# A fused attention and mixture-of-experts kernel: the last segment's maximum, the late loads, the zero fills and the written-out order are changed

## The chip, the cores and the metric

The kernel runs on one core of a Trainium2 chip. The metric is the device time of one execution in microseconds (us). Its engines are TensorE (PE; its weight loads are PEld), VectorE (DVE), ScalarE (ACT), GpSimd (POOL) and SyncE (SP, which issues the loads and stores). Each engine works through its own queue in order.

## The reference

The input is x, 4 batches of 11456 tokens with 128 channels, float32. First comes an attention with 32 inducing points, then a mixture of 8 experts with 4 slots each, in which every token goes to every slot with a weight ("soft" routing).

```python
def mab(q, kv):
    s = scale * (q @ kv.transpose(0, 2, 1))
    s = s - s.max(-1, keepdims=True)
    a = np.exp(s)
    a /= a.sum(-1, keepdims=True) + 1e-09
    return a @ kv
h = mab(I, x)                       # per batch: 32 inducing points look at the tokens
x = mab(x, h)                       # tokens look at the 32 rows of h
...
logits = x @ phi                    # tokens x 32 slots
d = np.exp(logits - logits.max(0)); d /= d.sum(0) + 1e-09
slot_input = d.T @ x                # softmax over all tokens of all batches
h = np.maximum(slot_input[e] @ w1[e], 0.0); slot_out[e] = h @ w2[e]
c = np.exp(logits - logits.max(1)); c /= c.sum(1) + 1e-09
return c @ slot_out                 # softmax over the slots
```

## The kernel before

The 4 batches are cut into 6 tiles each, so there are 24 tiles n of up to 15 blocks of 128 tokens; names below carry the tile's number. Work goes in three passes.

**First pass, per tile.** x is loaded twice (L282, L294): `xn` as it lies and `xt` transposed (tiles 0 to 5 are transposed on TensorE instead). TensorE multiplies `xt` with the inducing points (s1p, L329), VectorE takes maxima, ScalarE exponentiates, VectorE transposes in 32 x 32 blocks (e1), and TensorE accumulates exp(s)·x per batch (ha, L405). After a batch's six tiles, `first_out` normalises to h (hs, htp, hts, bdg; L453 to L476).

**Second pass, `second(n)` per tile.** Scores of tokens against h (s2p, L329, needs `xt` again), VectorE transposes them (bts, L576) and takes the maximum over the 32 (bmx, L579), GpSimd subtracts it (`bt_n`, L583), ScalarE exponentiates (L586), TensorE transposes back (tt, L592) and multiplies with h·phi (lp, L605), which gives the logits and their divisor; VectorE divides into the logit buffer l_all (L624, the last block by ScalarE, L629/L631), and GpSimd multiplies `bt` with the reciprocal divisor (bml, L635).

**Segments.** Three tiles make a segment k (`segment(k)`, L661). Its maximum over all tokens is taken on VectorE (t1_k, L667; in the last two segments tile by tile, tm, L657), turned by TensorE (pt_k, L672), reduced (mc_k, L679), spread to all partitions by TensorE (pb_k, L682) and copied by ScalarE (m_all, L685). d_n = l − maximum is taken on VectorE for the tiles in the list DV, straight from pb_k, on GpSimd for the others, from the copy (L706); ScalarE exponentiates it (L709), and TensorE accumulates exp(d)ᵀ·bt over the segment into u_k (L719). DW lists the tiles whose d is written in the pair layout that the l_all reads have, the others in a plain one. Since each segment has its own maximum, the sums of the segments are weighted against each other afterwards (ws, wl; L777 to L822).

**Experts (`experts()`, L752).** From the u_k come the slot inputs (sit, L845 to L852, copied into the zero-filled buffer ma by z1s, L863), 128 products with w1 (hpm, L872), ReLU on ScalarE (L880), a transpose per half (htm, L885), copies on VectorE into the zero-filled ma and mb (z2, L890), 128 products with w2 (so, L901), the divisor (zpp, rz; sos, L908), and the result spread to all partitions (sr, L911; srs, L914). The zero fills are two memsets on GpSimd (L764 of 1440 columns, L774 of 1152). The weights (8 transfers of 960 KB and one of 512 KB, L741, L743) are the last loads.

**Third pass, `third(n)` and `output(n)`.** The softmax over slots on the logits (maxima cm, L511; subtraction, L517/L520; exponential, L524; half sums ch, L532; sums cz, L541 to L547; product and transpose, L967, L970), then products with srs (po, L1000), copies to ot by VectorE and ScalarE (L1011), and stores (L1020).

Small zero products (`fill`, L1057 to L1063, and L235) keep TensorE working at some places. The large x and weight tiles share a ring of 13 buffers; some x tiles lie instead in parts of l_all that are not yet written (XTAG, NTAG), and the first logits there wait until such a tile is used up. Each step is registered by `op(engine, cost, name, function, ...)`, and the order in which the steps are issued, on all engines and the DMA queue, is written out by hand as a string of pairs of characters (ORDER, L54), one pair per step. So nothing decides the order at build time, and each engine's queue is a subsequence of that string.

## Time and profile before

| | |
|---|---|
| runs | 217.27, 216.47, 216.58 us; median 216.58 |
| profiled execution | 217.6 us, of which the span of instructions is 215.5 |
| busy, share of the span | TensorE 188.7 us (88%), VectorE 162.6 (75%), ScalarE 135.5 (63%), GpSimd 125.5 (58%) |
| HBM | 49.84 MB read, 23.59 MB written, 341 GB/s over the span |

The span begins at 0 with the first instruction; all positions below are in us from there. "PEclk" is the share of full clock that TensorE was granted. A share of busy time over the whole span mixes stages, so the rows below go by stretches of time. Where a row says [0.65 <-ACT d L709], the engine was idle for 0.65 us ahead of it, and ScalarE's step at L709 ended that.

### The profile page before, as it was taken

What the parts mean: (1) busy time and instruction counts of PE and PEld (TensorE: products, weight loads), DVE (VectorE), ACT (ScalarE), POOL (GpSimd) and SP (SyncE); (2) the same over time, 40 slices, a digit from 0 to 9 for tenths busy, and PEclk for the clock granted to TensorE, in tenths of its full rate; (3) what the DMA queues carried; (4) which work ended last, traced back from release to release, by engine and by line L of the source; (5) the groups of instructions that cost most, each with busy time, mean ns of one, the idle gap of its engine ahead of it and who ended that gap; (6) DMA issues with size and microseconds to landing.
All of it is one profiled execution on the core that took longest, in us unless ns stands there. A gap on an engine that the chain in (4) does not pass through costs nothing.

```text
span 215.5 us, 6873 instructions
## 1 busy us (share of the span) xinstructions
PE 188.7 (88%) x2778; PEld 129.7 (60%) x2778; DVE 162.6 (75%) x375; ACT 135.5 (63%) x368; POOL 125.5 (58%) x138
## 2 busy tenths in 40 slices
...
GB/s 218 387 429 416 393 422 415 415 415 361 233 389 422 422 412 419 408 419 412 415 416 414 419 236 0 6 5 3 66 378 410 418 421 422 412 421 423 411 416 190
DMA packets 12799, 73.87 MB, mean 343 GB/s; under 512 B 1633, under 2 KB 2657, under 8 KB 12769
## 3 DMA queue, kind: packets, MB, share of 16 engines
...
q10 hardware_dynamic: 432, 0.17, 0.3%
...
HBM read 49.84 MB, written 23.59 MB: 341 GB/s over the span
## 4 chain that ended last, share of the span: by engine, by line
PE 59%; DMA 10%; DVE 9%; POOL 7%; issue 4%; ACT 3%; SPq 1%; DVEq 0%; ACTq 0%; POOLq 0%
PE po L1000 10%; PE s1p L329 9%; PE ha L405 9%; PE s2p L329 7%; DMA w<-w 6%; PE lp L605 6%; DMA xn<-xn 4%; DVE ot L1011 4%; PE tt L592 4%; PE tp L306 3%; POOL d L706 3%; PE hpm L872 2%; POOL bt L583 2%; PE u L719 2%; DVE l_all L970 2%
## 5 line engine op out<-in xcount | busy, mean ns | idle before, releaser
L1000 PE MATMUL po<-l_all,srs 32*128 32x480 f32 (+1 forms) x200 | 43.6, 746 | 3.8 <-DVE l_all L970 1.8
L1000 PEld LDWEIGHTS po<-l_all,srs 32*128 32x128 f32 x200 | 22.0, 229 | 24.4 <-ACT ot L1011 10.5
L1011 ACT COPY ot<-po 128x480 f32<-128x480 f32 (+1 forms) x65 | 31.8, 576 | 7.4 <-PE po L1000 7.1
L583 POOL TENSOR_TENSOR bt<-bt,bm 128x480 f32<-128x480 f32 x24 | 23.6, 1001 | 16.6 <-DVE bm L579 14.1
L967 POOL TENSOR_TENSOR ct<-ct,cz 128x480 f32<-128x480 f32 x24 | 23.7, 996 | 9.2 <-DVE cz L547 9.2
L605 PE MATMUL lp<-bdg,a2t 128*128 128x132 f32 x192 | 25.7, 278 | 0.6 <-ACT d L709 0.6
L340 DVE TENSOR_SCALAR_CACHE_REDUCE s<-s1p 128x480 f32<-128x480 f32 (+1 forms) x24 | 15.0, 644 | 14.2 <-PE s1p L329 13.8
L635 POOL TENSOR_TENSOR bt<-bt,bz 128x480 f32<-128x480 f32 x24 | 23.5, 1003 | 2.8 <-DVE bz L617 1.9
L605 PEld LDWEIGHTS lp<-bdg,a2t 128*128 128x128 f32 x192 | 23.3, 190 | 1.8 <-ACT d L709 0.8
L1011 DVE COPY ot<-po 128x480 f32<-128x480 f32 (+1 forms) x35 | 20.2, 602 | 3.3 <-PE po L1000 3.3
L706 POOL TENSOR_TENSOR d<-l_all,m_all 128x512 f32<-128x512 f32 x19 | 21.8, 1173 | 1.3 <-ACT m_all L685 1.3
L520 POOL TENSOR_TENSOR ct<-l_all,cm 128x512 f32<-128x512 f32 x18 | 18.8, 1053 | 3.9 <-DVE l_all L970 2.4
L405 PE MATMUL ha<-xn,e 128*32 128x128 f32 x570 | 19.6, 275 | 1.6 <-issue 1.5
L329 PE MATMUL s1p<-xt,it_sb 128*32 128x480 f32 x160 | 19.8, 571 | 0.8 <-ACT xt L314 0.7
L386 ACT ACTIVATE s<-s,negm 128x480 f32<-128x480 f32 (+1 forms) x24 | 16.6, 697 | 5.7 <-DVE negm L371 5.7
L329 PE MATMUL s2p<-xt,hts 128*32 128x480 f32 x160 | 19.6, 571 | 0.0
L405 PEld LDWEIGHTS ha<-xn,e 128*32 128x32 f32 x570 | 16.5, 109 | 4.1 <-issue 2.2
L709 ACT ACTIVATE d<-d 128x512 f32<-128x512 f32 x24 | 14.9, 633 | 5.9 <-POOL d L706 5.0
L342 POOL MEMSET s<- 128x16 f32 x4 | 0.5, 117 | 31.1 <-DVE e L389 30.8
L970 DVE STREAM_TRANSPOSE l_all<-ct 128x480 f32<-128x480 f32 x24 | 15.8, 660 | 1.9 <-POOL ct L967 1.9
L389 DVE STREAM_TRANSPOSE e<-s 128x480 f32<-128x480 f32 x24 | 15.6, 657 | 1.9 <-ACT s L386 1.7
L576 DVE STREAM_TRANSPOSE bt<-s2p 128x480 f32<-128x480 f32 x24 | 15.6, 665 | 0.8 <-PE s2p L329 0.4
...
## 6 DMA issues: line engine op xcount, KB each, us to landing
...
```

The source lines that it names most:

```text
L329: nc.tensor.matmul(dst[32 * g : 32 * g + 32, :w], lhs, src, start=True, stop=True)
L386: nc.scalar.activation(t[:, :v], t[:, :v], AF.Exp, bias=T["negm", b, g], accum_out=z6[:, a : a + 1])
L405: nc.tensor.matmul(ha[32 * q : 32 * q + 32, :P], T["e1", a][:, j * S : (j + 1) * S], T["xn", a][:, j * P : (j + 1) * P], start=c == lo and ...
L520: nc.gpsimd.tensor_tensor(t.rearrange("p (a e s) -> p a e s", s=S, e=2), l_blocks(n), m, op=ALU.subtract)
L583: nc.gpsimd.tensor_tensor(t, t, T["bm", n][:, :nb].unsqueeze(2).broadcast_to(full), op=ALU.subtract)
L605: nc.tensor.matmul(pt[:, q * 4 * SZ : (q * 4 + m) * SZ], t[: m * S, q * P : (q + 1) * P], bdgs[b % 2].rearrange("p q s -> p (q s)")[: m * ...
L635: nc.gpsimd.tensor_tensor(t, t, T["bz", n][:, :nb].unsqueeze(2).broadcast_to(full), op=ALU.mult)
L706: e.tensor_tensor(t.rearrange(o, s=S, e=2), l_pairs(n), m, op=ALU.subtract)
L967: nc.gpsimd.tensor_tensor(t, t, T["cz", n][:, :nb].unsqueeze(2).broadcast_to([P, nb, S]), op=ALU.mult)
L970: nc.vector.transpose(l_of(n), T[ck][:, :w])
L1000: nc.tensor.matmul(ptile("mm", ("po", n, g, h))[:, : hi - lo], T["srs",][q, :], l_of(n)[q, lo:hi], start=True, stop=True)
L1011: (nc.vector.tensor_copy if dve else nc.scalar.copy)(T["ot", n][:, g * w + lo : g * w + hi], T["po", n, g, h][:, : hi - lo])
```

## The change

- **Last segment.** The column maxima mc_k are kept for all segments. Before pb_7 is spread, a new reduction on VectorE (nmc) takes the largest of all eight, so that pb_7 holds the maximum over all tokens. d_21, d_22 and d_23 subtract that; the copy m_all for segment 7 and the reduction nm go, the weights wl (now on VectorE, 64 wide, from pb_7) no longer cover segment 7, and u_7 is copied without a weight.
- **Subtractions.** d_20 goes from VectorE to GpSimd (DV); d_20 and d_22 are written in the plain layout (DW).
- **Zero fills.** Both go from GpSimd to ScalarE, as a product of ones with 0.
- **Loads.** xt_12 lies at the end of l_all instead of in the ring. 28 transfers (HS: xt 9 to 11 and 18 to 23, xn 6 and 14 to 23, w 0 to 7) are issued as two halves of 480 KB each.
- **Experts.** Each half of hpm and so is written as experts 0 to 3 and 4 to 7 instead of 0 to 5 and 6 to 7.
- **Fills on TensorE.** 13 zero products instead of 10: one early, five between u_17 and pt_7, three between u_18 and pb_7, two behind sit, two ahead of sr.
- **Order.** ORDER is another string. The loads keep their order; the compute steps and the stores do not.

The rest of the diff (a variant for tiles in a list XB, which is empty, and the host's reshaping) moves nothing.

```diff
-DV = [12, 20, 21, 22, 23]
-DW = [3, 9, 14, 20, 22]
+DV = [12, 21, 22, 23]
+DW = [3, 9, 14]
-XTAG = {9: 'xa', 10: 'xb', 15: 'xa', 16: 'xb'}
+XTAG = {9: 'xa', 10: 'xb', 15: 'xa', 16: 'xb', 12: 'xc'}
-NF = 10
+HS = [('t', 9), ('t', 10), ('t', 11), ('n', 6), ('t', 18),
...
+NF = 13
 ORDER = (
...
+                    for r in halves(("n", a)):
+                        nc.sync.dma_start(t[:, r], xn[a - 1][:, r])
...
-            nc.vector.tensor_reduce(stile("mc", ("mc", k))[:S], T["pt", k][:S, :w], axis=AX.X, op=ALU.max)
+            nc.vector.tensor_reduce(mc_all[:S, k : k + 1], T["pt", k][:S, :w], axis=AX.X, op=ALU.max)
...
+            mc = mc_all[:S, k : k + 1] if k < NSEG - 1 else T["nmc",][:S]
+            nc.tensor.matmul(ptile("mm", ("pb", k))[:, :S], mc.broadcast_to([S, P]), ident[:S, :S], start=True, stop=True)
...
+        def g1():
+            nc.vector.tensor_reduce(stile("nmc", ("nmc",), 1, 1)[:S], mc_all[:S], axis=AX.X, op=ALU.max)
...
-            nc.gpsimd.memset(ma[:, : 5 * ZW], 0.0)
+            nc.scalar.mul(ma[:, : 5 * ZW], ones.broadcast_to([P, 5 * ZW]), 0.0)
...
-            nc.gpsimd.memset(T["z2", 1], 0.0)
+            nc.scalar.mul(mb[:, : 4 * ZW], ones.broadcast_to([P, 4 * ZW]), 0.0)
...
         def g2():
-            nc.gpsimd.tensor_tensor(
-                blocks(stile("w2", ("wl",), W * S, 1)), blocks(m_last), T["nm",].unsqueeze(1).broadcast_to([P, W, S]), op=ALU.subtract,
-            )
+            pb = T["pb", NSEG - 1][:, :S].unsqueeze(1).broadcast_to([P, W, S])
+            nc.vector.tensor_tensor(blocks(stile("w2", ("wl",), W * S, 1)), blocks(m_last), pb, op=ALU.subtract)
...
         def g5():
-            nc.vector.tensor_tensor(us_all[:, last], T["u", NSEG - 1][:, :S], T["wl",][:, (W - 2) * S : (W - 1) * S], op=ALU.mult)
+            (nc.vector.tensor_copy if G5 == "DVE" else nc.scalar.copy)(us_all[:, last], T["u", NSEG - 1][:, :S])
...
-        parts = (range(0, 6), range(6, E))
+        parts = (range(0, 4), range(4, E))
```

How the order moves is seen at three places. The first is GpSimd's queue around the first step of tile 18: `bt` is scores less maximum (L583, then L616) or times reciprocal (L635, then L682), `d` is logits less segment maximum. Before:

```order
L635 TENSOR_TENSOR bt_15_1503<-bt_15_1503,bz_15_1793 128x480
L635 TENSOR_TENSOR bt_16_1584<-bt_16_1584,bz_16_1869 128x480
L635 TENSOR_TENSOR bt_17_1661<-bt_17_1661,bz_17_1886 128x480
L583 TENSOR_TENSOR bt_18_1939<-bt_18_1939,bm_18_1942 128x480
L706 TENSOR_TENSOR d_13_1974<-l_all_78,m_all_79 128x512
L706 TENSOR_TENSOR d_14_1976<-l_all_78,m_all_79 128x8x32x2
L583 TENSOR_TENSOR bt_19_1954<-bt_19_1954,bm_19_1958 128x480
L583 TENSOR_TENSOR bt_20_1956<-bt_20_1956,bm_20_1960 128x480
L774 MEMSET mb_2096 128x1152
L583 TENSOR_TENSOR bt_21_2068<-bt_21_2068,bm_21_2072 128x480
L583 TENSOR_TENSOR bt_22_2070<-bt_22_2070,bm_22_2076 128x480
L583 TENSOR_TENSOR bt_23_2074<-bt_23_2074,bm_23_2078 128x480
```

With the change:

```order
L682 TENSOR_TENSOR bt_14_1547<-bt_14_1547,bz_14_1776 128x480
L682 TENSOR_TENSOR bt_16_1626<-bt_16_1626,bz_16_1849 128x480
L682 TENSOR_TENSOR bt_17_1701<-bt_17_1701,bz_17_1903 128x480
L775 TENSOR_TENSOR d_13_1945<-l_all_78,m_all_79 128x512
L775 TENSOR_TENSOR d_14_1992<-l_all_78,m_all_79 128x8x32x2
L616 TENSOR_TENSOR bt_18_1980<-bt_18_1980,bm_18_1982 128x480
L616 TENSOR_TENSOR bt_19_1984<-bt_19_1984,bm_19_1988 128x480
L616 TENSOR_TENSOR bt_20_1986<-bt_20_1986,bm_20_1990 128x480
L682 TENSOR_TENSOR bt_15_1549<-bt_15_1549,bz_15_1778 128x480
L616 TENSOR_TENSOR bt_21_2050<-bt_21_2050,bm_21_2101 128x480
L616 TENSOR_TENSOR bt_22_2103<-bt_22_2103,bm_22_2105 128x480
L682 TENSOR_TENSOR bt_18_1980<-bt_18_1980,bz_18_2108 128x480
```

d_13 and d_14 now stand ahead of bt_18, the product of tile 15 behind bt_20, the memset of mb is gone, and the subtractions and products of tiles 18 to 23 are interleaved.

The second is TensorE's queue at the same time, where pt_4, pb_4 are the turned and the spread maximum of segment 4 (tiles 12 to 14). Before:

```order
L605 MATMUL lp_17_1880<-bdg0_88,a2t_17_1860 128x132 x3
L605 MATMUL lp_17_1880<-bdg0_88,a2t_17_1860 128x99
L672 MATMUL pt_4_1888<-cst_70,t1_4_1872 32x128
L329 MATMUL s2p_18_1899<-xt_18_911,hts_3_1876 32x480 x4
L719 MATMUL u_3_1836<-d_10_1653,bt_10_1002 32x32 x15
L329 MATMUL s2p_19_1919<-xt_19_913,hts_3_1876 32x480 x4
L719 MATMUL u_3_1836<-d_11_1733,bt_11_1117 32x32 x15
L682 MATMUL pb_4_1944<-cst_70,mc_4_1897 128x32
```

With the change:

```order
L727 MATMUL pt_4_1896<-cst_70,t1_4_1855 32x128
L640 MATMUL lp_17_1898<-bdg0_89,a2t_17_1846 128x132 x3
L640 MATMUL lp_17_1898<-bdg0_89,a2t_17_1846 128x99
L481 MATMUL htp_3_1905<-cst_70,hs_3_1894 128x128
L738 MATMUL pb_4_1915<-cst_70,mc_all_80 128x32
L788 MATMUL u_3_1736<-d_10_1694,bt_10_1020 32x32 x15
L346 MATMUL s2p_18_1950<-xt_18_965,hts_3_1921 32x480 x4
```

pt_4 now stands ahead of lp_17, and pb_4 ahead of s2p_18.

The third is ScalarE's queue at the end of the chain, from d_21's exponential on. Before:

```order
L709 ACTIVATE d_21_2376<-d_21_2376 128x512
L709 ACTIVATE d_22_2380<-d_22_2380 128x512
L709 ACTIVATE d_23_2382<-d_23_2382 128x512
L819 ACTIVATE wl_2389<-wl_2389 128x96
L728 COPY us_all_82<-u_6_2313 128x32
L880 ACTIVATE ma_2391<-hpm_0_2468 128x128
L524 ACTIVATE ct_8_2510<-ct_8_2510 128x480
```

With the change:

```order
L778 ACTIVATE d_21_2401<-d_21_2401 128x512
L778 ACTIVATE d_22_2403<-d_22_2403 128x512
L778 ACTIVATE d_23_2405<-d_23_2405 128x512
L884 ACTIVATE wl_2408<-wl_2408 128x64
L799 COPY us_all_83<-u_6_2331 128x32
L836 ACTIVATE ma_2470<-ones_87 128x1440
L540 ACTIVATE ct_9_2480<-ct_9_2480 128x480
```

The copy of pb_7 (further up) is gone, and the zero fill of ma, read from ones, stands behind us_6's copy and ahead of the exponentials of the third pass.

## Rows read from the trace of the kernel before

**Rows 1.** Stretches: length, busy PE, PEld, DVE, ACT, POOL (instructions), clock, DMA share, GB/s.

```profile
12.00:104.00 92.00, 91.82 (x1516) 64.31 (x1518) 78.86 (x192) 61.26 (x178) 52.98 (x56) 1.00 0.99 400
...
117.00:139.00 22.00, 21.42 (x444) 16.71 (x443) 21.50 (x45) 17.48 (x54) 21.72 (x23) 1.00 0.47 190
139.00:154.00 15.00, 13.50 (x351) 11.48 (x348) 12.26 (x32) 4.83 (x15) 12.40 (x17) 0.89 0.02 4
...
160.00:200.00 40.00, 36.91 (x150) 18.27 (x144) 30.86 (x65) 32.27 (x74) 24.63 (x26) 0.74 1.02 417
```

**Rows 2.** Timeline of the DMA queue: start, us, what, count.

```profile
54.52 0.33 SPq L294 DMA_DIRECT2D l_all<-xt  x1
```

**Rows 3.** Timeline of GpSimd: start, us, what, count, idle before.

```profile
116.94 1.00 POOL L583 TENSOR_TENSOR bt<-bt,bm 128x480 f32<-128x480 f32 x1 [0.90 <-DMA w<-w]
118.22 2.31 POOL L706 TENSOR_TENSOR d<-l_all,m_all 128x512 f32<-128x512 f32 x2 [0.28 <-ACT m_all L685]
...
122.36 1.07 POOL L774 MEMSET mb<- 128x1152 f32 x1
...
135.82 2.93 POOL L635 TENSOR_TENSOR bt<-bt,bz 128x480 f32<-128x480 f32 x3
...
139.02 1.32 POOL L764 MEMSET ma<- 128x1440 f32 x1
```

**Rows 4.** Timeline of TensorE, 104 to 147 us.

```profile
108.98 1.84 PE L405 MATMUL ha<-xn,e 128*32 128x128 f32 x57
...
114.34 1.01 PE L329 MATMUL s2p<-xt,hts 128*32 128x480 f32 x8
...
116.65 0.40 PE L682 MATMUL pb<-cst,mc 32*128 32x32 f32 x2
...
139.68 0.89 PE L719 MATMUL u<-d,bt 128*32 128x32 f32 x60 [0.65 <-ACT d L709]
...
142.10 4.61 PE L872 MATMUL hpm<-w,ma 128*32 128x128 f32 x112
146.64 0.33 PE L885 MATMUL htm<-cst,ma 128*128 128x128 f32 x1
```

**Rows 5.** Timeline of VectorE, 124 to 139 us.

```profile
124.53 1.70 DVE L667 TENSOR_REDUCE t<-l_all 128x32 f32<-128x1536 f32 x1
...
136.94 0.69 DVE L706 TENSOR_TENSOR d<-l_all,pb 128x512 f32<-128x512 f32 x1 [0.42 <-ACT m_all L685]
137.55 0.26 DVE L811 TENSOR_REDUCE nm<-m_all 128x32 f32<-128x96 f32 x1
137.72 1.60 DVE L706 TENSOR_TENSOR d<-l_all,pb 128x512 f32<-128x512 f32 x2
```

**Rows 6.** Timeline of ScalarE, 138 to 141 us.

```profile
138.91 1.16 ACT L709 ACTIVATE d<-d 128x512 f32<-128x512 f32 x2 [0.61 <-DVE d L706]
...
140.14 0.16 ACT L728 COPY us_all<-u 128x32 f32<-128x32 f32 x1
```

**Rows 7.** Groups of ScalarE by shape: busy us, mean ns, idle before.

```profile
L709 ACT ACTIVATE d<-d 128x512 f32<-128x512 f32 x24 | 14.9, 633 | 5.9 <-POOL d L706 5.0 <-DVE d L706 0.6 <-POOL s L342 0.2
...
L785 ACT ACTIVATE mb<-mb 128x192 f32<-128x192 f32 x1 | 0.4, 375 | 0.0
```

**Rows 8.** Busy time by stretch, around the experts and first stores.

```profile
141.50:144.90 3.40, 3.40 (x60) 2.98 (x61) 3.40 (x8) 0.00 (x0) 3.25 (x5) 0.50 0.03 7
144.90:146.70 1.80, 1.80 (x65) 1.60 (x58) 0.43 (x1) 1.22 (x3) 1.80 (x2) 1.00 0.00 0
158.00:166.00 8.00, 7.61 (x42) 3.84 (x42) 7.49 (x17) 7.77 (x20) 4.29 (x5) 1.00 1.02 408
```

**Rows 9.** Timeline of all engines after the experts.

```profile
151.64 0.35 DVE L908 TENSOR_SCALAR sos<-so,rz_l 128x128 f32<-128x128 f32 x1 [0.15 <-PE so L901]
...
153.68 0.89 ACT L1011 COPY ot<-po 128x240 f32<-128x240 f32 x3 [0.84 <-PE po L1000]
```

**Rows 10.** Groups by shape, VectorE.

```profile
L511 DVE TENSOR_REDUCE cm<-l_all 128x16 f32<-128x512 f32 x24 | 15.8, 660 | 0.0
```

More of the change, by code (lines that the diff above doesn't have):

```diff
@@ L79, with tw, gw @@
 FREE_RINGS = ()
-DYN = ("mm", "half", "x")
+DYN = ("mm", "half", "x", "a2t")
 def width(n):
     return SIZES[n % NCH] * S
+def tw(n):
+    return LW if n in XB else width(n)
+def gw(n):
+    return [LW, LW, LW, LW - P] if n in XB else [width(n)] * 4
 def valid(n):
@@ L276, in load, with halves @@
         assert not {tag_of("xn", a), tag_of("xt", a)} & taken
+        def halves(n):
+            w = XW // 2 if n in HS else XW
+            return [slice(o, o + w) for o in range(0, XW, w)]
         def ldn(lo, hi):
@@ L289, in load @@
         for lo, hi in zip(cuts, cuts[1:]):
[L290 removed]
+            op("DMA", 2.50 * (hi - lo) / 2048 + 0.05 * (("n", a) in HS) + (1.9 if a == 0 and not lo else 0.0), ("ldn", a, lo), ldn(lo, hi), (), [("xn", a, lo)], [] if lo else [(tag_of("xn", a), ("xn", a))])
         if a in HOST_T:
             def ldt():
[L294 to L296 removed]
+                t = xtile("xt", a)
+                for r in halves(("t", a)):
+                    nc.sync.dma_start(t[:, r], xt_d[HOST_T.index(a)][:, r])
+            op("DMA", 2.50 * nb / 16 + 0.05 * (("t", a) in HS), ("ldt", a), ldt, (), [("xt", a)], [(tag_of("xt", a), ("xt", a))])
             return
@@ L503, in soft @@
     def soft(pre, n, src, half, key):
-        w, nb = width(n), SIZES[n % NCH]
-        full = (P, nb, S)
+        w, nb = tw(n), tw(n) // S
         mk, zk = (pre + "m", n), (pre + "z", n)
@@ L562, in a2_of @@
     def a2_of(n):
-        return T["bt", n][:, : width(n)]
+        return T["bt", n][:, : tw(n)]
     def second(n):
@@ L576, in bts, with bcp, btx @@
             nc.vector.transpose(wtile("s2", ("bt", n))[:, :w], T["s2p", n][:, :w])
+        def bcp():
+            t = wtile("a2t", ("s2c", n), LW)
+            nc.scalar.copy(t[:, :sw], T["s2p", n][:, :sw])
+            nc.scalar.copy(t[:, sw:], T["s2p", n][:, sw - S : sw])
+        def btx():
+            pt = ptile("mm", ("tx", n))
+            for q in range(4):
+                nc.tensor.transpose(pt[:, q * P : (q + 1) * P], T["s2c", n][:, q * P : (q + 1) * P], ident)
         def bmx():
-            nc.vector.tensor_reduce(stile("bm", ("bm", n), JM, RINGS["bm"])[:, :nb], blocks(a2_of(n)), axis=AX.X, op=ALU.max)
+            src = T["tx", n] if n in XB else a2_of(n)
+            nc.vector.tensor_reduce(stile("bm", ("bm", n), LW // S, RINGS["bm"])[:, :nb], blocks(src), axis=AX.X, op=ALU.max)
         def bsb():
+            if n in XB:
+                if ("xbt",) not in T:
+                    btile("x", ("xbt",))
+                i = XB.index(n)
+                T["bt", n] = T["xbt",][:, i * LW : (i + 1) * LW]
             t = blocks(a2_of(n))
-            nc.gpsimd.tensor_tensor(t, t, T["bm", n][:, :nb].unsqueeze(2).broadcast_to(full), op=ALU.subtract)
+            e, src = (nc.vector, blocks(T["tx", n])) if n in XB else (nc.gpsimd, t)
+            e.tensor_tensor(t, src, T["bm", n][:, :nb].unsqueeze(2).broadcast_to(full), op=ALU.subtract)
         def bxp():
@@ L960, in third @@
     def third(n):
-        w, nb = width(n), SIZES[n % NCH]
+        w, nb = tw(n), tw(n) // S
         ck = ("ct", n)
@@ L988, in output @@
     def output(n):
-        w = width(n)
+        ws = gw(n)
+        w, at = ws[0], [sum(ws[:g]) for g in range(5)]
         cuts = [0, w // 2, w] if n == HEAD else [0, w]
         parts = list(zip(cuts, cuts[1:]))
+        assert n != HEAD or n not in XB
         for h, (lo, hi) in enumerate(parts):
@@ L1094 @@
             xt[HOST_T.index(a), :, : nb * P] = part.transpose(3, 0, 2, 1).reshape(C, nb * P)
-    def cut(t):
-        return np.ascontiguousarray(t.reshape(-1, P, H, XW // H).transpose(0, 2, 1, 3))
     w1 = inputs["moe_w1"].transpose(1, 0, 2)
```

187 lines of the change are left out of this document (108 added, 79 removed).

## The prediction

> **What bounds the kernel now.** I read the stages first, then the engine timelines of the stretch where no stage is full, then the clock. The busy times by stretch [rows 1] show three stages. From 12 to 104 us TensorE works 91.82 of 92.00 us and the DMA engines are at 0.99, so both are full; the change takes no product out of that stage, so nothing can be won there, and a stall of TensorE would add one for one. From 160 to 200 us the stores run at 1.02 of the DMA engines and 417 GB/s; the bytes stay, so that stage only starts earlier or later. Between lies a chain: the DMA share falls to 0.47 (117 to 139 us) and to 0.02 (139 to 154 us). What is won or lost there moves the stores and so the end.
>
> In the chain GpSimd is busy 21.72 of 22.00 us from 117 to 139 [rows 1]: from bt_18 at 116.94 to the last of the bt·bz products at 135.82 + 2.93 = 138.75 [rows 3], 21.81 in all. VectorE is the second candidate: its last two subtractions (1.60 from 137.72) release ScalarE's last two exponentials, which end at 138.91 + 1.16 = 140.07 [rows 5, 6]. u_23 waits for that; `u` ends at 139.68 + 0.89 = 140.57, and the experts' first product comes at 142.10 [rows 4]. So before the change the VectorE-ScalarE chain ends last, 1.3 us behind GpSimd. Whoever shortens it by more meets GpSimd.
>
> **The change part by part.**
>
> *Loads.* 28 transfers are cut in two, and xt_12 goes to the end of the logit buffer. The queue still stops at xt_15, issued at 54.52 once s2p_9 has left its place in that buffer [rows 2], which is not changed; and TensorE is full meanwhile. I cost this part at 0, the 28 further issues (0.33 each on a queue that mostly waits) with it. The cover: loads have no gain to give while TensorE is the bound, and the weights, last in the queue, are first needed at 142. What speaks against it is the rate: halves of the same size in the stores, 158 to 166 us, moved at 408 GB/s [rows 8] beside 417 [rows 1], 2.2% less. On the 20 halved x loads (20 × 0.98 MB at 417 GB/s = 47 us) that is 1.0 us of lateness. From 117 us on 22 × 190 GB/s = 4.2 MB come [rows 1], 10 us at full rate, so the 8.39 MB of weights end at 127 and the last x tile lands 20 us before, at 107; the products of the last two tiles run from 108.98 [rows 4], so 2 us are to spare and 1.0 costs nothing. The Trainium skill ("DMA: Bandwidth & Descriptors", its rule on batching) asks for at least 1 MiB per transfer for three quarters of the peak, which speaks against halves; taken as a quarter lost on those 47 us (an estimate from that page), the last x tile would come some 14 us too late and the sum be 230. This case's 960 KB transfers lie under that size too and move at 417 GB/s, so the rows decide.
>
> *Zero fills.* The fill of 1152 columns (GpSimd, 1.07) [rows 3] goes to ScalarE far earlier, where ScalarE is busy 61.26 of 92.00 us [rows 1]; it stands ahead of an exponential and of hs_2, and would cost up to its own length if TensorE waited for hs_2. I take 0. The fill of 1440 columns goes from GpSimd (1.32) [rows 3] to ScalarE, behind the last exponentials. No row shows such a fill on ScalarE. 192 columns took 0.375 and 512 took 0.633 [rows 7], 0.81 ns per column, which carried on gives 0.633 + 928 × 0.81 ns = 1.38. Below stands GpSimd's 1.32, above a price in proportion, 0.633 × 1440/512 = 1.78. I take 1.38, as the two rows are ScalarE's own.
>
> *GpSimd in the chain.* From bt_18 on it loses the fill (1.07) and d_13 and d_14 (2.31 [rows 3], now ahead of bt_18), and gains the product of tile 15 (0.98) and d_20 (1.16): 21.81 − 1.07 − 2.31 + 0.98 + 1.16 = 20.57. But the maximum t1_5 (1.70 on VectorE at 124.53 [rows 5]) now stands ahead of bts_21, so bt_21 and its neighbours come late. Counted through the two orders with the row durations, GpSimd idles about 1.9 (0 if VectorE is ahead, 2.8 if every bt waits). pb_4, now ahead of s2p_18, I put at about 114, so that d_13 and d_14 (2.31, and 0.3 to 0.5 for the copy) leave bt_18 at 116.85. GpSimd's end: 116.85 + 20.57 + 1.9 = 139.3, 0.55 later than before.
>
> *VectorE and ScalarE in the chain.* Gone ahead of d_23: nm (0.26) [rows 5], the copy of pb_7 that d_21 waited for (0.42 of idle) [rows 5], d_20 (0.91, as d_22 now: 1.60 − 0.69) less a transpose of 0.66 (an estimate from a cm of the same width [rows 10]) that takes its place (0.25), and 0.2 by which the plain layout shortens d_22 (0.91 to 0.69 [rows 5]). Added: the new maximum over 8 numbers, 0.2 (bounds 0.1 and the 0.26 of nm). So d_23's exponential ends at 140.07 − 0.26 − 0.42 − 0.25 − 0.2 + 0.2 = 139.1. u_23 then waits for GpSimd: 139.3 + 0.45 (half of `u`'s 0.89) = 139.75, 0.8 earlier than 140.57. us_7 no longer waits for the weight, which is worth about 0.1. The fill of 1440 ends at 139.1 + 0.23 (two short steps, which end at 140.30 now [rows 6]) + 1.38 = 140.7, about when the slot inputs (sit) are there. **First expert product: 0.9 earlier** (1.3 at best; 0 if the fill takes 1.78 and GpSimd idles 2.8).
>
> *Experts.* Before, TensorE hardly waits between the first expert product at 142.10 and sos at 151.64 [rows 4, 9], since each transpose htm stands behind other products. Now htm_1 follows all of hpm at once: it waits for the hand-over (sos idled 0.15 for such a one [rows 9]) and ReLU (0.375 or less, ScalarE's 192-column row [rows 7]), of which htm_0 (0.33 [rows 4]) covers most: +0.2. One break in the stream of products fewer gives back 0.1. **+0.1** (−0.2 to +0.4).
>
> *First stores.* Ahead of the first output copies VectorE gets two maxima cm, and ScalarE the sum cz_11 that hangs on them. Before, ScalarE's copy began 153.68 − 151.64 = 2.04 behind sos [rows 9]. Now sos 0.35, two cm of 0.66 [rows 10] and cz, a sum of at most that size, make 2.33 for VectorE alone, 0.3 more; cz_11 sums half a tile, so I take **+0.2** (0 to +0.6), all of it on the path, as the stores are the bound from there on.
>
> *The fills of TensorE* (13 for 10) stand at waits that end elsewhere: 0; each is two records of at most htm's 0.33 [rows 4], and were none of the 3 covered it would be 2 × 3 × 0.33 less their overlap, 1 us.
>
> **Sum:** −0.9 + 0.1 + 0.2 = −0.6. The profiled execution took 217.6 (span 215.5), so 217.0; the runs' median, 216.58, lies 1.0 below it, so **216.0**. A measurement of this kernel can tell some 0.5%, 1.08 us: faster means under 215.50, slower over 217.66.
>
> **The rivals.**
>
> *The clock stays full: 214.7.* TensorE's granted clock is 0.50 from 141.50 to 144.90, the 1.2 GHz level, and 1.00 right after [rows 8]. In the slow stretch 60 records took 3.40, 57 ns each; in the fast one 65 took 1.80, 28 ns. The fall followed a thin stretch, u_23's wait of 0.65 [rows 4] and the short slot-input products. About 53 expert products ran slow, 53 × 25 ns = 1.3. If the later and fuller u products and the fills keep the clock up, that goes: 216.0 − 1.3. For it: the waits ahead of the experts get shorter. Against it: the same two fills stand behind sit, the u products stay short, and GpSimd keeps TensorE waiting instead. The Trainium skill ("TensorE: Matmul & The Clock Gate", Part 1) says that the throttled state is the default and activity releases it; this trace agrees, as the clock rose only while the expert products ran, and by that the thin stretch would recur and my sum stand.
>
> *The late pb_4: 217.9, slower.* pb_4 now stands ahead of s2p_18 on TensorE, and d_13, d_14 ahead of bt_18 on GpSimd; before, s2p_18 began at 114.34 and pb_4 only at 116.65 [rows 4]. If t1_4, pt_4 and mc_4 don't come earlier, pb_4 stays there and s2p_18 waits 2.7. Then d_13 starts at 117.1, bt_18 at 119.5, and GpSimd ends at 119.5 + 20.57 + 1.0 (fewer gaps, as VectorE catches up) = 141.1; u_23 ends at 141.5, 1.0 late: 216.58 + 1.0 + 0.3 = 217.9. It decides from a pb_4 at about 116.4. For it: the row of pb_4, and a full VectorE. Against it: VectorE's maximum t1_4 is moved forward, and pt_4 ahead of lp_17.
>
> *The change gives nothing: 216.9.* The chain only changes hands: GpSimd, with d_20 added, idles 2.8 and ends 0.9 later than I put it, or ScalarE's fill takes 1.78 behind later exponentials; the first expert product stays at 142.10 and the 0.3 of the later steps remain.
>
> *The halves hold up the last x tile: 217.5.* Were the loss three times that of the 408 GB/s row, 3.0 us, the tile would be 1.0 late, and with it `u` and the rest of the chain. Against it stands the row itself.
>
> **How the numbers follow.** The forecast gets 0.45, with a range of its own of 215.2 to 217.0, a third of it below 215.50. The clock rival gets 0.25, nearly all of it faster; the late pb_4 0.18, three quarters of it slower; no gain 0.10, a fifth of it slower; the halves 0.02, half of it slower. Faster: 0.15 + 0.24 = 0.39. Slower: 0.14 + 0.02 + 0.01 = 0.17. Same: 0.44. The range goes from the clock's 214.7 with another 0.7 of chain gain to the late pb_4's 217.9.
>
> **What would show it.** Right: stages as before up to 104 us with TensorE full; pb_4 near 114; GpSimd's last product near 139.3, d_23's exponential near 139.1; the ScalarE fill near 1.4; first expert product near 141.2; 9.6 us from there to the last one; first copies 2.2 to 2.3 behind sos. The clock's fate is the row of the stretch after sit. Wrong: TensorE idle before 104 us (a halved load or hs_2 late), s2p_18 behind a waiting pb_4, first expert product at or behind 142.1, or a store stage below 410 GB/s.

## The result, and the profile after

| | before | with the change |
|---|---|---|
| median of 20 runs each | 217.30 us (216.07 to 218.87) | 216.12 us (212.79 to 217.29) |
| ratio | 1 | 0.9881, 95% interval 0.9846 to 0.9916 |
| profiled execution | 217.6 (span 215.5) | 215.5 (span 213.4) |

The ratio counts only runs within 1.5% of the fastest run of their kernel: beside one run of 212.79 us these are eight of the changed kernel's twenty and all twenty of the other's, so it overstates the gain, and the quotient of the medians, 0.9946, is used here. The kernel is faster by 1.2 us at the medians, 0.5%; two later comparisons gave 1.7 and 1.8 us, 0.8%. The forecast was 216.0 us, with 0.44 for no measurable change and 0.39 for faster, and the measured median lies 0.1 beside it. That it lies so near is luck: the forecast was a gain of 0.6 from a median of 216.58, and the measured gain is 1.2 from a median of 217.30. The way there is not the one that the prediction's sum took, and two of its terms were of the wrong size.

The stretches of the changed kernel, columns as in [rows 1]:

```profile
12.00:104.00 92.00, 91.72 (x1515) 64.39 (x1516) 79.23 (x191) 62.53 (x180) 53.56 (x56) 1.00 0.99 394
...
117.00:139.00 22.00, 21.39 (x497) 17.57 (x497) 20.93 (x47) 17.13 (x53) 21.02 (x24) 1.00 0.57 225
139.00:154.00 15.00, 14.26 (x326) 11.90 (x312) 13.39 (x34) 8.11 (x20) 13.67 (x17) 1.00 0.13 43
...
160.00:200.00 40.00, 34.89 (x141) 16.96 (x138) 29.68 (x59) 31.40 (x70) 21.65 (x23) 0.72 1.02 417
```

The first stage is as full as before, and the store stage runs at the same 417 GB/s. What differs lies between. ScalarE does 8.11 us of work from 139 to 154 where it did 4.83 [rows 1], the difference being the zero fill (0.94 of it) and the exponentials and output copies that come earlier. TensorE's clock is 1.00 over that stretch where it was 0.89.

TensorE's timeline in the chain of the changed kernel, to be held against [rows 4]:

```profile
113.39 0.40 PE L738 MATMUL pb<-cst,mc_all 32*128 32x32 f32 x2
114.00 1.82 PE L346 MATMUL s2p<-xt,hts 128*32 128x480 f32 x16
...
138.68 0.45 PE L788 MATMUL u<-d,bt 128*32 128x32 f32 x30 [0.29 <-ACT us_all L799]
...
139.75 0.69 PE L245 MATMUL fill<-srs 128*128 128x128 f32 x4
140.37 3.70 PE L937 MATMUL hpm<-w,ma 128*32 128x128 f32 x128
144.00 0.33 PE L950 MATMUL htm<-cst,ma 128*128 128x128 f32 x1
```

pb_4 came at 113.39, 3.26 earlier than in [rows 4], so d_13 and d_14 found it ready. `u` ends at 138.68 + 0.45 = 139.13 (before 140.57), the first expert product comes at 140.37 (before 142.10), and its layer takes 3.70 for 128 records where 112 took 4.61. The row's "ACT us_all" is a copy from the same time; the product could not start before GpSimd's last product, whose timeline, beside [rows 3], is:

```profile
117.37 2.91 POOL L616 TENSOR_TENSOR bt<-bt,bm 128x480 f32<-128x480 f32 x3
120.23 1.00 POOL L682 TENSOR_TENSOR bt<-bt,bz 128x480 f32<-128x480 f32 x1
121.87 0.99 POOL L616 TENSOR_TENSOR bt<-bt,bm 128x480 f32<-128x480 f32 x1 [0.64 <-PE u L788]
123.12 0.99 POOL L616 TENSOR_TENSOR bt<-bt,bm 128x480 f32<-128x480 f32 x1 [0.25 <-DVE bm L606]
...
135.71 2.91 POOL L682 TENSOR_TENSOR bt<-bt,bz 128x480 f32<-128x480 f32 x3
```

Its last product ends at 135.71 + 2.91 = 138.62. The two gaps that the transpose behind t1_5 makes are there, 0.64 and 0.25, so 0.9 and not the 1.9 that I had counted. VectorE and ScalarE, beside [rows 5, 6]:

```profile
134.72 0.15 DVE L747 TENSOR_REDUCE nmc<-mc_all 32x1 f32<-32x8 f32 x1
...
135.79 1.96 DVE L775 TENSOR_TENSOR d<-l_all,pb 128x512 f32<-128x512 f32 x3 [0.52 <-PE pb L738]
```

```profile
136.63 1.79 ACT L778 ACTIVATE d<-d 128x512 f32<-128x512 f32 x3
138.33 0.24 ACT L884 ACTIVATE wl<-wl 128x64 f32<-128x64 f32 x1
138.47 0.17 ACT L799 COPY us_all<-u 128x32 f32<-128x32 f32 x1
138.53 1.40 ACT L836 ACTIVATE ma<-ones 128x1440 f32<-128x1440 f32 x1
```

The three exponentials end at 138.42, where two ended at 140.07 [rows 6]. The new maximum took 0.15. The zero fill of 1440 columns took 1.40 on ScalarE (1.38 was forecast) and ended at 139.93.

Absolute positions shift by up to 2 us from one execution to the next, and the shift is there by s2p_18, which began between 113.73 and 115.80 in thirteen of the fourteen profiles that there are. From s2p_18 to sos, though, the same kernel repeats to a few hundredths as long as its clock does. So the readings below count from s2p_18.

### The profile page after: what moved, and what is told of

Its sections match the earlier page's. It is cut to its first block, busy times and chain, and to the rows that moved or that the text cites. A ratio compares the mean times of both kernels' runs of the same rounds, so it can differ in the third digit from the quotient of the medians.

```text
span 213.4 us, 6928 instructions
## 1 busy us (share of the span) xinstructions
PE 189.8 (89%) x2784; PEld 130.5 (61%) x2784; DVE 163.2 (76%) x375; ACT 138.4 (65%) x369; POOL 123.6 (58%) x136
## 4 chain that ended last, share of the span: by engine, by line
PE 68%; DVE 12%; DMA 4%; issue 4%; POOL 2%; ACT 2%; SPq 1%; ACTq 0%; DVEq 0%; POOLq 0%
PE ha L422 11%; PE lp L640 10%; PE s2p L346 9%; PE s1p L346 9%; PE po L1065 8%; PE tt L625 5%; DMA xn<-xn 4%; DVE ot L1078 4%; PE tp L323 3%; PE u L788 3%; DVE l_all L1033 2%; PE so L966 2%; PE hpm L937 2%; DVE cz L557 2%; DVE cm L527 1%
## 5 line engine op out<-in xcount | busy, mean ns | idle before, releaser
L1065 PE MATMUL po<-l_all,srs 32*128 32x480 f32 (+1 forms) x200 | 44.7, 735 | 6.6 <-ACT ot L1078 3.0
L616 POOL TENSOR_TENSOR bt<-bt,bm 128x480 f32<-128x480 f32 x24 | 23.7, 998 | 13.2 <-DVE bm L606 12.3
L775 POOL TENSOR_TENSOR d<-l_all,m_all 128x512 f32<-128x512 f32 x20 | 23.2, 1165 | 2.0 <-ACT m_all L741 1.8
L682 POOL TENSOR_TENSOR bt<-bt,bz 128x480 f32<-128x480 f32 x24 | 23.7, 998 | 0.3 <-DVE bz L658 0.3
L346 PE MATMUL s1p<-xt,it_sb 128*32 128x480 f32 x152 | 18.4, 572 | 0.7 <-ACT xt L331 0.7
L346 PE MATMUL s2p<-xt,hts 128*32 128x480 f32 x152 | 17.8, 569 | 0.0
L540 ACT ACTIVATE ct<-ct 128x480 f32<-128x480 f32 x24 | 14.5, 618 | 4.5 <-POOL ct L533 3.2
```

What stands on the lines that cost most here:

```text
L346: nc.tensor.matmul(dst[32 * g : 32 * g + 32, :w], lhs, src, start=True, stop=True)
L616: e.tensor_tensor(t, src, T["bm", n][:, :nb].unsqueeze(2).broadcast_to(full), op=ALU.subtract)
L682: nc.gpsimd.tensor_tensor(t, t, T["bz", n][:, :nb].unsqueeze(2).broadcast_to(full), op=ALU.mult)
L775: e.tensor_tensor(t.rearrange(o, s=S, e=2), l_pairs(n), m, op=ALU.subtract)
L1065: nc.tensor.matmul(ptile("mm", ("po", n, g, h))[:, : min(hi, ws[g]) - lo], T["srs",][q, :], l_of(n)[q, lo : min(hi, ws[g])], start=True, s ...
```

## Experiments

All twelve were run in four batches, each beside runs of the kernel before on the same chip; the median of before was 217.41 us in the first batch (32 runs), 217.25 in the second (29), 217.51 in the third (29) and 217.24 in the fourth (17). The changed kernel itself ran in the first and the third batch only.

| from s2p_18's start (us) | `u` ends | first expert product | from there to sos | sos to end of span | clock in the first layer |
|---|---|---|---|---|---|
| before | 26.23 | 27.76 | 9.54 | 63.9 | 0.50, then 1.00 |
| before, again (2nd batch) | 26.20 | 27.47 | 8.19 | 63.7 | 1.00 |
| changed | 25.13 | 26.37 | 8.13 | 64.9 | 1.00 |
| changed, again (1st batch) | 25.15 | 26.39 | 8.13 | 64.0 | 1.00 |
| changed, third (3rd batch) | 25.15 | 26.39 | 8.13 | 64.2 | 1.00 |

### The kernels as they are, again

> The changed kernel once more, as the yardstick of this batch. Both theories: 1.0 to 1.5% under the kernel before, the first expert product near 140.4 us, the granted clock 1.00 over the first layer of the experts, the first output copy near 150.8, and a hole in the stores between 154 and 156 us.

> The changed kernel once more, as the yardstick of this batch: s2p_18 to the first expert product 26.4 us, hpm to sos 8.1, clock 1.00 there, the hole in the stores again two to four us behind the first one.

> The kernel before once more, for a second look at its clock. If the half clock over the first layer of the experts belongs to this order of work, it shows 0.50 again for 3 to 3.5 us from about 141.5; if it came by chance, 1.00. The first expert product at 142.1 plus or minus 0.7.

The changed kernel's median was 215.72 in the first batch (ratio 0.9916, 0.9881 to 0.9951) and 215.67 in the third (0.9919, 0.9869 to 0.9968), so the gain came out at 0.8%, under the 1.0 to 1.5 expected. All three of its profiles show the clock at 1.00 over the layer, and the table shows how alike they are up to sos. The kernel before did not repeat its half clock. In its second profile TensorE's timeline and the stretch behind it are these:

```profile
139.18 0.89 PE L719 MATMUL u<-d,bt 128*32 128x32 f32 x60 [0.65 <-ACT d L709]
...
140.72 0.69 PE L235 MATMUL fill<-srs 128*128 128x128 f32 x4
141.34 3.26 PE L872 MATMUL hpm<-w,ma 128*32 128x128 f32 x112
```

```profile
142.00:144.00 2.00, 2.00 (x83) 2.00 (x79) 2.00 (x4) 0.28 (x1) 2.00 (x3) 1.00 0.04 12
```

The same 112 records took 3.26 here and 4.61 in [rows 4], the same four fill records 0.69 and 0.95. So the half clock is no fixed property of the kernel before; it befalls some of its executions. It then costs 27.76 − 27.47 = 0.3 ahead of the layer and 9.54 − 8.19 = 1.35 up to sos.

The record also has the mean granted clock of every run. Of the 107 runs of the kernel before in the four batches, the 44 with a mean of 0.919 or more have a median of 216.58 us and none is above 218.08; the 63 with less have 218.21 and go up to 221.69. The changed kernel's 41 runs (median 215.97) show no such tie: those above 216.8 us have means from 0.911 to 0.932. So in the kernel before the longer runs go with a low clock. Where in the span the clock was low these means do not say, since the store stage has long stretches of half clock too (0.74 from 160 to 200 us, [rows 1]).

### Do the further zero products keep the clock up?

```diff
-        op("PE", 0.22, ("fill", k), fill(k), [("eps0",)], [("fill", k)], [("mm", ("fill", k))], ni=4)
+        op("PE", 0.22, ("fill", k), (lambda: None) if k in [6, 7, 8] else fill(k), [("eps0",)], [("fill", k)], [("mm", ("fill", k))], ni=4)
```

> The changed kernel without the three zero products between u_18 and pb_7. Theory 'fills' (the three further products keep TensorE's clock up over the experts' first layer): the first expert product stays at 140.4, but the clock shows 0.50 over the first 3 us of that layer, and the time is 1.0 to 1.4 us above the changed kernel's. Theory 'short waits' (the clock stayed up because the waits ahead of the experts got shorter): the clock stays 1.00 there and the time is within 0.4 us of the changed kernel's.

Median 216.84 us (215.11 to 220.48), 1.1 above the changed kernel of the batch; ratio 0.9963 (0.9924 to 1.0002). The profile shows the clock at 1.00 over the layer and the first expert product 26.41 behind s2p_18, as with the fills (the stretch over the layer):

```profile
142.00:144.00 2.00, 2.00 (x84) 2.00 (x76) 2.00 (x4) 1.11 (x2) 2.00 (x5) 1.00 0.03 8
```

So the time is that of "fills", the profile that of "short waits", and neither theory is shown. With a fall of the clock that befalls only some executions both can be: one profile is one execution. The runs are spread over 5.4 us, where the changed kernel's nine of this batch lie within 1.4 (215.20 to 216.64), but its twenty of the first comparison within 4.5. The five runs above 217.5 us have mean clocks of 0.909 to 0.922 and the seven others 0.922 to 0.931, which speaks for the clock. Against it stands that the kernel with whole loads (below), which keeps these three fills, has a median 1.0 above the changed kernel's in the same batch too.

```diff
-NF = 10
+NF = 13
...
+        j = q.index(at['f9', 3])
+        q[j:j] = [at['fill', k] for k in (10, 11, 12)]
```

> The kernel before, with three further zero products ahead of pb_7 and nothing else. Theory 'fills': the clock is 1.00 over the first layer of the experts, which still begins at 142.1; sos comes at 150.3 to 150.6 and not at 151.6, and the time is 1.0 to 1.4 us below the kernel before. Theory 'short waits': the clock shows 0.50 there as before, and the time is within 0.5 us of the kernel before.

Median 218.13 us, ratio 1.0013 (0.997 to 1.0057): no gain. (The step f9, 3 is the product just ahead of pb_7; at gives a step's number by its name, q is the order.) Its one profile is of a run of 227.73 us, with the clock at 0.85 from 12 to 148 us, so it says nothing of that layer. Three zero products ahead of pb_7 by themselves do not help the kernel before.

```diff
-NF = 10
+NF = 14
...
+        for k, x in ((10, ('f9', 3)), (11, ('c2', 20)), (12, ('c2', 22)), (13, ('c2', 22))):
+            j = q.index(at[x])
+            q[j:j] = [at['fill', k]]
```

> The kernel before with four zero products in the waits between pb_7 and u_22 (one ahead of pb_7, one ahead of u_20, two ahead of u_22). Theory 'thin stretch' (the clock falls in some executions because TensorE has little to do from pb_7 to sit): the clock is 1.00 over the first layer of the experts, hpm to sos takes 8.2 and not 9.5 us, and the median over the rounds is 0.3 to 1.0 us below the kernel before, with no run above 218.5. Theory 'chance' (the fall has nothing to do with that stretch): the median is within 0.3 us of the kernel before.

Median 216.62 us (215.79 to 218.19) beside 217.51 (215.65 to 220.78) for the kernel before in the same batch, 0.9 lower. Of the latter's 29 runs 13 lay above 218.19, the highest of the 12 runs here. The clock was 1.00 and the layers took 8.19 from the first expert product to sos (TensorE's timeline, then the stretch over the layer):

```profile
142.33 3.26 PE L876 MATMUL hpm<-w,ma 128*32 128x128 f32 x112
```

```profile
142.00:144.00 2.00, 2.00 (x65) 1.88 (x67) 2.00 (x5) 0.00 (x0) 2.00 (x3) 1.00 0.05 12
```

The fills cost 0.2 (`u` ends 26.43 behind s2p_18). What goes is the upper half of the runs. The ratio, 0.9978 (0.9938 to 1.0017), doesn't exclude no change; the theory "thin stretch" rests on the medians and the highest runs, which came as it had said, and not on the ratio. Nor is it shown that the clock is what changed: seven of the 12 runs have a mean clock under 0.919, as 63 of the 107 of the kernel before have, and the kernel before without these fills has a profile at 1.00 as well.

### Is the new maximum worth anything?

```diff
+        q.insert(q.index(at['h3', 7]) + 1, at['h4', 7])
+        q.insert(q.index(at['ds', 21]) + 1, at['g1',])
...
-            mc = mc_all[:S, k : k + 1] if k < NSEG - 1 else T["nmc",][:S]
+            mc = mc_all[:S, k : k + 1]
```

> The changed kernel with the last segment's own maximum as before: pb_7 from mc_7, a copy for segment 7, nm behind d_21, weights 96 wide, u_7 weighted. Theory 'path' (the new maximum shortened the chain): d_23's exponential ends 0.4 to 0.8 us later against pb_7, the first expert product comes 0.5 to 0.9 us later, and the time is 0.5 to 1.0 us above the changed kernel's (1.3 more if the clock falls). Theory 'order' (order and zero fills did it): the first expert product within 0.2 us of pb_7 plus 5.1.

ScalarE's timeline of this kernel, then VectorE's:

```profile
136.47 0.17 ACT L745 COPY m_all<-pb 128x32 f32<-128x32 f32 x1
...
137.39 0.63 ACT L783 ACTIVATE d<-d 128x512 f32<-128x512 f32 x1 [0.53 <-DVE d L780]
138.22 1.23 ACT L783 ACTIVATE d<-d 128x512 f32<-128x512 f32 x2 [0.20 <-DVE d L780]
```

```profile
136.67 0.69 DVE L780 TENSOR_TENSOR d<-l_all,pb 128x512 f32<-128x512 f32 x1 [1.37 <-ACT m_all L745]
137.28 0.26 DVE L751 TENSOR_REDUCE nm<-m_all 128x32 f32<-128x96 f32 x1
137.45 1.27 DVE L780 TENSOR_TENSOR d<-l_all,pb 128x512 f32<-128x512 f32 x2
```

d_21 waits for the copy of pb_7 again, and nm stands between. The last exponential ends at 139.45, 25.32 behind s2p_18; in the changed kernel it is 24.42 (138.42 − 114.00). So the maximum is worth 0.90 on ScalarE's end, of which u_23 gets what GpSimd's end leaves (24.63 here, 24.62 in the changed kernel): 25.32 − 24.62 = 0.70. In this execution the clock was 0.50 from 139 us, and the first expert product came 28.47 behind s2p_18. The median, 215.98 us, with a ratio of 0.9927 (0.9885 to 0.9969), cannot be told from the changed kernel's; its runs go from 213.77 to 218.89. So theory "path" is shown in the trace, and the 0.5 to 1.0 us that it expected in the time are not there; why not stays open.

### Does it matter where the zero fill stands?

```diff
+        i = [at[x] for x in [('g0',)]]
+        q = [x for x in q if x not in i]
+        j = q.index(at[('bml', 23)]) + 1
+        q[j:j] = i
...
-            nc.scalar.mul(ma[:, : 5 * ZW], ones.broadcast_to([P, 5 * ZW]), 0.0)
+            nc.gpsimd.memset(ma[:, : 5 * ZW], 0.0)
```

> The changed kernel with the fill of 1440 columns back on GpSimd, behind its last bt product. Theory 'fill on the path': the fill takes 1.32 us, u_6's weighting on GpSimd waits for it, and with it the slot inputs: the first expert product 0.6 to 1.0 us later, the time as much above the changed kernel's. Theory 'fill hidden': the first expert product within 0.2 us of the changed kernel's.

Median 218.23 us, ratio 1.0024 (0.9978 to 1.007): the whole gain is gone. The timelines of TensorE and GpSimd:

```profile
139.58 0.41 PE L915 MATMUL sit<-sis,cst 128*128 128x32 f32 x2
140.65 0.41 PE L919 MATMUL sit<-us_all,h 128*128 128x32 f32 x2 [0.66 <-POOL us_all L896]
...
141.31 1.20 PE L250 MATMUL fill<-srs 128*128 128x128 f32 x4
142.44 4.60 PE L942 MATMUL hpm<-w,ma 128*32 128x128 f32 x128
```

```profile
139.07 1.31 POOL L841 MEMSET ma<- 128x1440 f32 x1
140.33 0.26 POOL L896 TENSOR_TENSOR us_all<-us_all,wl 128x32 f32<-128x32 f32 x1
```

`u` ends as in the changed kernel (25.15 behind s2p_18), but u_6's weighting now waits behind the fill, and TensorE for it, 0.66. The first expert product comes 27.94 behind s2p_18, 1.6 late: 0.66 of wait, and the rest at a clock that fell to 0.50 right behind that wait (four fill records 1.20 for 0.69). From there to sos it takes 9.03 for 8.13. The fill was on the path as soon as `u` came earlier; the expectation of 0.6 to 1.0 left the clock out.

### Do the halved loads do anything?

```diff
-HS = [('t', 9), ('t', 10), ('t', 11), ('n', 6), ('t', 18),
...
+HS = []
```

> The changed kernel with its 28 halved loads whole again. My reading, that the loads carry no time here: the load rate goes from about 405 back to 415 GB/s after 70 us, the last weights land about 2 us earlier, TensorE's products come at the same times within 0.5 us, and the time is within 0.5 us of the changed kernel's. Rival, that earlier halves let products start earlier: TensorE gets idle time before 112 us and the time rises by 0.5 to 1.5 us.

Median 216.75 us, 1.0 above the changed kernel's 215.72 in the batch and outside the 0.5 that I expected; the ratio, 0.9933 (0.9894 to 0.9972), is not to be told from the changed kernel's 0.9916. The rate of the loads, changed kernel first, whole loads second:

```profile
80.00:104.00 24.00, 24.00 (x479) 17.13 (x469) 23.80 (x57) 16.84 (x51) 19.91 (x21) 1.00 1.03 406
```

```profile
80.00:104.00 24.00, 23.37 (x469) 16.16 (x469) 22.84 (x55) 15.71 (x46) 18.98 (x21) 1.00 1.01 414
```

The halves cost 2% of the rate, as the 408 GB/s in the stores had said [rows 8], and nothing of the way to sos: the first expert product comes 26.38 behind s2p_18 with whole loads, and 26.37 to 26.39 with halves. What this profile has longer lies behind sos (65.2 us to the end of the span, for 64.0 to 64.9), so the 1.0 us of the median is not put down to the loads. The last weights landed later for it (225 GB/s from 117 to 139 us, 191 with whole loads), and were not needed. The 0.6 of idle in the second row are waits of TensorE for which the profile names nothing ("issue", 0.92 in one piece); the changed kernel without the three fills, which has the halves, shows the same 0.91, so the rival is not borne out either. The Trainium skill's rule on batching ("DMA: Bandwidth & Descriptors"), at least 1 MiB for three quarters of the peak, does not describe these loads: transfers of 480 KB moved at 406 GB/s, 98% of the rate of whole ones.

### Where the rest of the gain went: the first stores

The change reached sos 1.16 us sooner, counted from s2p_18 and with the clock full in both (34.50 for 35.66), but the span ends 99.4, 98.6 and 98.7 us behind s2p_18 in its three profiles, for 99.3 in the second profile of the kernel before: 0.1 later to 0.7 sooner. The stores of the changed kernel, pairs of us from 152:

```profile
152.00:154.00 2.00, 2.00 (x17) 1.07 (x9) 2.00 (x5) 1.83 (x4) 1.67 (x3) 1.00 0.88 300
154.00:156.00 2.00, 1.99 (x14) 0.90 (x12) 2.00 (x5) 1.52 (x4) 0.16 (x1) 1.00 0.51 173
156.00:158.00 2.00, 1.28 (x9) 0.46 (x9) 2.00 (x5) 0.90 (x3) 1.25 (x2) 1.00 1.10 442
158.00:160.00 2.00, 2.00 (x16) 1.36 (x15) 1.65 (x4) 1.63 (x4) 1.16 (x2) 1.00 0.96 384
```

and of the second profile of the kernel before:

```profile
152.00:154.00 2.00, 1.70 (x12) 0.95 (x16) 2.00 (x6) 1.61 (x5) 2.00 (x3) 1.00 0.49 156
154.00:156.00 2.00, 2.00 (x18) 0.90 (x12) 2.00 (x5) 2.00 (x5) 1.88 (x3) 1.00 1.00 334
156.00:158.00 2.00, 2.00 (x17) 1.22 (x13) 2.00 (x6) 1.76 (x6) 0.55 (x1) 1.00 1.06 417
158.00:160.00 2.00, 2.00 (x10) 0.81 (x6) 1.71 (x4) 2.00 (x6) 1.21 (x2) 1.00 1.02 415
```

The stores begin 0.9 earlier in the changed kernel (151.18 for 152.09) but run half empty from 154 to 156. By 160 us it has moved 2 × (4 + 300 + 173 + 442 + 384) = 2606 KB, the kernel before 2 × (156 + 334 + 417 + 415) = 2644. The hole is not equally deep each time. Over the first 12 us behind sos the changed kernel's three profiles moved 234, 257 and 256 GB/s and the two of the kernel before 272 and 273; at 417 GB/s that is 1.1, 0.5 and 0.5 us less work done, about what the table's last column has more.

It is not the copies that are late: those of tile 0 end 5.5 us behind sos in all three profiles, and 5.6 in the kernel before. An issue on the DMA queue is. This is the fourth store in the changed kernel and, behind it, in the second profile of the kernel before:

```profile
152.92 1.65 SPq L1091 DMA_DIRECT2D out<-ot  x1
```

```profile
153.89 0.41 SPq L1020 DMA_DIRECT2D out<-ot  x1
```

Behind the 1.65 us the store of tile 0 was issued 6.17 us behind sos, for 5.59 in the kernel before. In the changed kernel's two other profiles one issue took 0.83 and 1.05 us, without the three fills 2.00 and with whole loads 1.97, and those two have the longest ends of the kernels that keep the changed order (65.4 and 65.2 us behind sos). Why an issue takes so long there is not shown.

```diff
+        mv = [('csm', 11), ('ctr', 10), ('cep', 11), ('crc', 11), ('cmx', 16), ('cml', 11)]
+        q = [x for x in q if self.ops[x][2] not in mv]
+        j = q.index(at['oe', 1, 1, 1]) + 1
+        q[j:j] = [at['ctr', 10]]
+        j = q.index(at['oe', 0, 1]) + 1
+        q[j:j] = [at[x] for x in (('csm', 11), ('cep', 11), ('cmx', 16), ('crc', 11), ('cml', 11))]
```

> The changed kernel with the sum cz_11 (and what hangs on it), the transpose of tile 10 and the maximum cm_16 moved behind the output copies of tiles 1 and 0. My reading, that part of the chain's gain is given back by first stores that wait for VectorE: the first copies come 0.2 us sooner behind sos, the hole in the stores two to five us after the first one closes (DMA share over 0.85 in each such pair of us), and the time falls 0.4 to 1.0 us below the changed kernel's. Rival, that the stores catch up anyway: within 0.2 us of the changed kernel's, with the store stage ending as early.

Median 217.40 us, ratio 0.9995 (0.9956 to 1.0035): a miss, 1.7 above the changed kernel's 215.7 of the other batches. The first copies did come sooner (1.96 behind sos for 2.29), but the hole stayed (214 GB/s from 154 to 156) and a second one opened: from 12 to 20 us behind sos the stores moved 349 GB/s, with TensorE busy all the time at 0.52 of its clock, where the changed kernel has 418 at 1.00. For the first hole ScalarE's timeline shows why:

```profile
154.21 0.60 ACT L547 ACTIVATE ct<-ct 128x480 f32<-128x480 f32 x1 [1.55 <-POOL ct L540]
154.72 1.00 ACT L1085 COPY ot<-po 128x480 f32<-128x480 f32 x2
```

The copies of tile 0 stand behind an exponential of tile 13 that waits for GpSimd, and begin 5.66 behind sos, for 4.29 in the changed kernel. In this order it is that exponential's place in ScalarE's queue that holds the store of tile 0, and I had moved VectorE's steps.

```diff
...
+        q = q[: q.index(at['ge',]) + 1] + [at[x] for x in tail]
```

> The changed kernel up to sos, and from there on the order of the kernel before (copies of the first tiles ahead of the sums of the later ones, po_4, po_9 and so on as there; cm_15 and cm_16 behind the copies of tile 10). Theory 'given back in the first stores' (the change reaches sos 1.1 us sooner, counted from s2p_18, but both kernels have moved the same bytes by 160 us): the DMA share is 0.9 or more in each pair of us from 154 on, the stores end 0.7 to 1.2 us sooner against sos than in the changed kernel, and the time is 0.6 to 1.2 us below the changed kernel's. Rival 'stores are limited elsewhere': the bytes moved nine us behind the first store are the same as the changed kernel's and the time is within 0.4 us of it.

The stores of this kernel by pairs of us:

```profile
152.00:154.00 2.00, 1.76 (x16) 0.84 (x14) 2.00 (x5) 1.82 (x5) 0.76 (x1) 1.00 0.72 242
154.00:156.00 2.00, 2.00 (x18) 1.17 (x15) 2.00 (x5) 1.55 (x4) 1.04 (x2) 1.00 1.11 404
```

(tail is the list of the remaining steps in the order of the kernel before; ge is sos.) Here the copies of tile 0 begin 3.56 behind sos, for 4.29 (152.79 − 148.50) in the changed kernel, the store of tile 0 is issued 5.10 behind sos, and the hole is gone (284 GB/s over the 12 us behind sos). The span ends 63.4 behind sos, for 64.0 to 64.9. The median is 215.14 us, 0.5 below the changed kernel's 215.67 of the same batch and the lowest of the study; the ratios, 0.9914 (0.9877 to 0.9952) and 0.9919, don't separate the two. So about half of what I had expected, and near the rival's bound: that this order closes the hole is shown, that it makes the kernel faster is not. Near the end, at 200 to 202 us, the stores of this order ran at 307 GB/s, with TensorE's clock at 0.50.

```diff
-NF = 13
+NF = 34
+        for k, x in [(13, ('po', 18)), (14, ('po', 18)), (15, ('po', 18)), (16, ('po', 17)),
...
+            q.insert(q.index(at[x]), at['fill', k])
```

> The changed kernel up to sos with the store order of the kernel before, and three zero products ahead of each of the last seven tiles' products po (21 in all). In that order without them the clock shows 0.50 from 196 us on, the last copies end at 200.5 and the stores run dry for half a us at 200 to 202. Theory 'clock at the end': with the zero products the clock is 1.00 from about 185 to 198, the last copies end 0.7 to 1.3 us sooner against sos, the dry half us goes, and the time is 0.3 to 0.6 us below that order's 215.1. Rival 'bytes bind': the clock rises and the last copies come sooner, but the time is within 0.2 us; or the zero products delay the copies by taking PSUM buffers, and the time rises by 0.3 us or more.

The end of this kernel's stores by stretch:

```profile
196.00:200.00 4.00, 3.51 (x23) 1.67 (x23) 2.85 (x6) 1.48 (x3) 1.37 (x2) 1.00 0.85 349
200.00:202.00 2.00, 1.96 (x14) 1.06 (x14) 0.09 (x1) 0.00 (x1) 0.00 (x0) 1.00 1.04 430
202.00:204.00 2.00, 0.00 (x0) 0.00 (x0) 2.00 (x4) 1.94 (x4) 0.00 (x0) 1.00 0.04 15
```

Median 216.63 us, 1.5 above the order without them, which ran in the batch before: the clock rose to 1.00, as wanted, and the last copies came later, 54.0 behind sos (to 204.3) for 51.3. The rival's second half held: a zero product waits its turn in the queue and for a buffer (0.25 us for a copy of VectorE at 194.68), and the last tiles' products stand behind it.

## Why the prediction was right, and where it wasn't

**The stages and the place.** Right. TensorE full up to 104 us, the DMA engines full at 417 GB/s from 160, and all of the difference in between.

**The chain.** Right in its mechanism. GpSimd and the VectorE-ScalarE chain ended nearly together (138.62 and 138.42), as the sum had them (139.3 and 139.1). The term was undersized: `u` ends 1.07 earlier from s2p_18 (25.14 for 26.21), not 0.8. GpSimd idled 0.9 and not 1.9, though bt_18 began 0.5 later than I had put it (117.37 for 116.85), so two errors partly cancel. The new maximum is the larger part of the 1.07: 0.90 on ScalarE's end, of which 0.70 reached u_23. The fill on ScalarE took 1.40 for the 1.38 that the two rows of other widths gave. That it left GpSimd was worth more than the tie that I saw in it, as u_6's weighting had stood behind it: 0.66 of wait when it was put back.

**The experts.** The term of +0.1 had the wrong sign: 8.13 for 8.19 with the clock full in both, so −0.06. The wait of htm_1 that I priced is there, and the broken stream before cost as much.

**The clock.** The step that failed: "the thin stretch would recur and my sum stand". I took the half clock for a property of this order of work, present before and after, and gave its absence 0.25. The runs showed a fall that befalls the kernel before in some executions (one profile of two) and was in none of the changed kernel's three. Its price is near the forecast: 1.35 for 1.3, and 0.3 more ahead of the layer (the forecast's 25 ns a record should have been 57 − 28 = 29, which makes 1.5). So the gain in the clock goes into the median as a share of it, and the measured gains, 1.2 to 1.8 us, lie between the sum's 0.6 and the rival's 1.9. That the thin stretch behind pb_7 is what invites the fall is supported, not shown: four zero products in it took the upper half of the runs of the kernel before away, and in the two variants of the changed kernel with longer waits ahead of the experts (the fill back on GpSimd, the last segment's own maximum) the one profile of each shows the half clock. The Trainium skill ("TensorE: Matmul & The Clock Gate", Part 1) has the throttled state as the default, which activity releases; the rows agree, as the clock came back to 1.00 at 144.90 while the expert products ran [rows 8].

**The first stores.** The term of +0.2 was right where it looked (sos to the first store 2.68 for 2.55) and looked too short: the loss came behind the first store, where an issue on the DMA queue took 0.83 to 1.65 us, for a reason that stays open. From sos to the end of the span the changed kernel takes 64.0 to 64.9 for 63.7 to 63.9, so 0.1 to 1.2 in all.

**The sum.** With the clock full in both, −1.1 in the chain, −0.1 in the experts and +0.7 in the stores (64.4, the mean of three, for 63.7) make −0.5, close to the −0.6 that I had by −0.9, +0.1 and +0.2: errors that cancel. The measured change of the medians, −1.2, has the clock's share on top, by this account. The runs fit it: beside the 44 runs of the kernel before with the higher mean clock (median 216.58) the changed kernel's 41 (215.97) are 0.6 lower.

**The rivals.** The late pb_4 didn't come: 113.39, before s2p_18, since t1_4 and pt_4 had been moved with it. The halves held up nothing on the way to sos.
